# Loading the first twelve weight tiles six at a time, and storing decoded weights six tiles late

## The chip, the cores and the metric

One core of a Trainium2 chip runs the whole program. The metric is the device time of one execution in microseconds (us), the median over several runs. The engines are TensorE (PE, with its weight loads as PEld), VectorE (DVE), ScalarE (ACT), GpSimd (POOL) and SyncE (SP), which here only issues DMA transfers.

## What is computed

The program is an attention with a compressive memory, followed by two feed-forward layers. The first twelve weight tiles belong to the first feed-forward layer, `moe`.

```python
scores = q @ k.T / sqrt(D); a = softmax(causal(scores)); local = a @ v      # B 4, H 8, S 576, D 64
mem_out = (phi(q) @ M_prev) / (phi(q) . z_prev + 1e-6)
x = g * mem_out + (1 - g) * local                                           # x: 2304 tokens x 512
h = x @ w_in;  x = (h * sigmoid(h)) @ w_out                                 # moe:  512 -> 2048 -> 512
gt = x @ w_gate; val = x @ w_val; out = (gt * sigmoid(gt) * val) @ w_out    # moe2: 512 -> 1536 -> 512
```

The weights arrive as 64-bit numbers.

## The kernel before, in words

**Attention.** Batch 0 is computed first, in eight units: four units A (a pair of heads, the first 256 rows) and four units B (the same pairs, the other 320 rows). Batches 1 to 3 follow, a pair of heads at a time. A unit B transposes `q_t` and `k_t` on PE (`psq`, `psk`, L367), multiplies them (`pss`, L434 and L509), takes row minima on DVE (L486, L510, closed by L515), exponentials on ACT (L490, L516), scales the rows on POOL (L523, five instructions), transposes the result on PE (`pst`), copies it to SBUF, and multiplies it with v into `U` (L619). ACT and DVE turn `U` into the token block `x` (L214, L342).

**First feed-forward layer.** Its 2048 hidden columns are cut into four slices of 512. Batch 0 gives two token blocks, A (256 tokens) and B (320 tokens). `order` in `CFG` gives the sequence of block and slice: A0 A1 B1 B0 A2 B2 A3 B3; the other tokens follow in blocks of 432. For one block and slice PE computes four `h` tiles (L870), ACT, DVE and POOL turn each into the pair `gh`, `gl` (L877, L878, L214, L880), and four `y` tiles follow (L928).

**Weight tiles.** A slice needs eight tiles: four of `w_in`, four of `w_out`. A tile is loaded as 512 KB of raw 64-bit words (L717 for `w_in`, L748 for `w_out`), decoded to 32 bits by ACT (L731) and DVE (L732, L733), and split into a high half (ACT, L214 `w<-raw`) and a low half (POOL, L773) in a buffer `w` of the pool `wp`, which has eight. The decoded pair is then stored to DRAM (L796, `wd<-w`, 512 KB) because later blocks load it from there (L759). Slice 0 is tiles 1 to 4 (`w_in`) and 5 to 8 (`w_out`), slice 1 is tiles 9 to 12 and 13 to 16, and so on. Tile 9 takes the buffer `w` of tile 1, so it needs that tile's matmuls and its store done.

`Prep.step` (L790) does one tile: it splits the oldest loaded one, loads ahead to two raw tiles, and issues the store of the tile that it has just split. The raw tiles share three buffers (`raw8=3`).

**What sets the order.** The program is written as a stream of steps; a scheduler with its own cost table merges them into one fixed order per engine. Each engine and SP's queue then run their list in order. A wait at the head of a list holds everything behind it.

Of the kernel before, what the change touches and what calls it, by code (L numbers as in the profile page):

```python
# [13 lines left out]
I32 = mybir.dt.int32  # L14
# [3 lines left out]
P = 128  # L18
BIG = 1.0e9
CFG = dict(  # L20
    raw8=3,
    raw=3,
    g=1,
    th=2,
    ps_m=3,
    ps_a=dict(A=5, B=5, G=5),
    ps_s=dict(),
    run=3000,
# [18 lines left out]
    ahead=2,  # L47
# [7 lines left out]
    pt=4,  # L55
    rate=0.55,
    late=0.6,
    ring=16,
    y0=36,
    jit=1,  # L60
# [33 lines left out]
def kernel(  # L94
# [34 lines left out]
    def f(ap):  # L129
        return ap.bitcast(F32)  # L130
# [20 lines left out]
    kp = kept.enter_context(tc.tile_pool(name="kp", bufs=1))  # L151
    pha = ExitStack()
    rawp = pha.enter_context(tc.tile_pool(name="rawp", bufs=CFG["raw"], side="right"))
    cur, ph2 = {"raw": rawp}, {}
# [191 lines left out]
    def unit(u):  # L346
# [202 lines left out]
        def T_A():  # L549
# [8 lines left out]
            o["ta"] = ta  # L558

        def T_B(step):  # L560
            own4()
            if step == 0:
# [114 lines left out]
    for u, key in enumerate(units):  # L677
        step, stages = unit(u)
        if u == NP:
            stages.insert(0, lambda: open_at("atB"))  # L680
            at_slot = max(slots) + 1
        if u == 2 * NP:
            stages.insert(0, open_F)
            at_slot = max(slots) + 1
        if CFG["stackb"] > 1 and u == NP * CFG["stackb"] + NP:
            stages.insert(0, open_G)
            at_slot = max(slots) + 1
        for i, st in enumerate(stages):
            slots.setdefault(at_slot + i, []).append(st)
        for sup in key[2]:  # L690
            ready[key[0], sup] = at_slot + len(stages)
        at_slot += step
# [14 lines left out]

    w1 = {}

    def load64(w, j, part, after=None):  # L710

        raw = cur["raw"].tile([P, 512, 2], I32, tag="raw8", name="raw8", bufs=CFG["raw8"])
        w2 = w.bitcast(I32)
        if after is not None:
            nc.gpsimd.tensor_copy(raw.bitcast(F32)[:, 0, 0:1], f(after))
        if part == 0:
            nc.sync.dma_start(  # L717
                out=raw.rearrange("p (k n) t -> p k (n t)", k=KD),
                in_=w2[:, 2 * P * j:2 * P * (j + 1)].rearrange("(k p) n -> p k n", p=P),
            )  # L720
        else:
            nc.sync.dma_start(out=raw.rearrange("p n t -> p (n t)"), in_=w2[P * j:P * j + P, :])
        return raw

    def decode(raw, t=None):
        hi, lo = raw[:, :, 1], raw[:, :, 0]
        u = hi.bitcast(F32)
        if t is None:
            t = cur["raw"].tile([P, 512], F32, tag="raw", name="raw", bufs=CFG["raw"])
        ti = t.bitcast(I32)  # L730
        nc.scalar.activation(out=t, in_=u, func=ACTF.Prelu, scale=2.0**-111, alpha=-(2.0**32))  # L731
        nc.vector.tensor_single_scalar(ti, ti, 3, op=ALU.logical_shift_left)  # L732
        nc.vector.scalar_tensor_tensor(ti, lo, 29, ti, ALU.logical_shift_right, ALU.bitwise_or)  # L733
        return t

    seen = {}

    def r_(ap):
        return ap.bitcast(F32R)

    def raw_w1(*key):
        if key in seen:
            return None
        if key[0] == 0:
            return load64(w1_in, key[1], 0)
        raw = cur["raw"].tile([P, 512, 2], I32, tag="raw8", name="raw8", bufs=CFG["raw8"])
        _, s, e = key
        nc.sync.dma_start(  # L748
            out=raw.rearrange("p (j n) t -> p j (n t)", j=NW),
            in_=w1_out.bitcast(I32)[P * NW * s:P * NW * (s + 1), 2 * P * e:2 * P * (e + 1)].rearrange(  # L750
                "(j p) n -> p j n", p=P
            ),
        )
        return raw

    def split_w1(t, key):
        if key in seen:
            w = wp.tile([P, 2, 512], F32, tag="w", name="w")
            nc.sync.dma_start(out=w, in_=seen[key])  # L759
            return r_(w[:, 0]), r_(w[:, 1])  # L760
        w = split_wp(decode(t), "1")
        seen[key] = dram.tile([P, 2, 512], F32, name="wd%d_%d" % (key[0], len(seen)))
        prep1.post.append((seen[key], w))
        return r_(w[:, 0]), r_(w[:, 1])

    def split_wp(t, kind):
        w = wp.tile([P, 2, 512], F32, tag="w", name="w")
        split_to(r_(w[:, 0]), r_(w[:, 1]), t, kind)
        return w
# [5 lines left out]
    class Prep:  # L775
        def __init__(self, load, split):
            self.load, self.split = load, split
            self.todo, self.raws, self.done, self.post = [], [], {}, []

        def add(self, keys):  # L780
            self.todo += keys
# [6 lines left out]
        def step(self, ahead=CFG["ahead"]):  # L788
            self.prefetch(1)
            if not self.raws:  # L790
                return
            key, t = self.raws.pop(0)
            self.done[key] = self.split(t, key)
            self.prefetch(ahead)
            for d, t in self.post:
                nc.sync.dma_start(out=d, in_=t)  # L796
            self.post = []

        def need(self, key):
            while key not in self.done:  # L800
# [3 lines left out]


    prep1 = Prep(raw_w1, split_w1)

    def token_block(key):
# [31 lines left out]
    def moe1():  # L840
        keys = []
        for n, sg in enumerate(segs):
            if n == 0 or sg["s"] != segs[n - 1]["s"]:
                keys.append(sg["s"])
        prep1.add([(0, j) for j in SLICES[keys[0]]] + [(1, keys[0], e) for e in range(KD)])
        yield ("init", 0)
        gs = [{} for _ in segs]
        fresh = [0]
# [56 lines left out]
        for n, sg in enumerate(segs):  # L905
            key, t0, nt, s = sg["key"], sg["t0"], sg["nt"], sg["s"]
# [14 lines left out]
            for e in range(KD):  # L921
                ps = bank("y")
                m, last = 0, 3 * len(SLICES[s]) - 1
                for wi, gi in ((0, 0), (1, 0), (0, 1)):
                    for ji, j in enumerate(SLICES[s]):
                        w, g = prep1.need((1, s, e))[wi], gs[n][j][gi]
# [43 lines left out]
    def prep_w2():  # L970
# [3 lines left out]
        def fetch(n):  # L974
            while todo and len(raws) < n and not ("hold" in ph2 and n > 1):
                j, part = todo.pop(0)
                raws.append(load64((w2_gate, w2_val, w2_out)[part], j, part // 2, gate[-2]))
# [423 lines left out]
    if True:  # L1401
        open_at("atA")
        setup_attn()
        load_A()
        setup()
        items = moe1()
        next(items)
        slot, n_g = 0, 0
# [92 lines left out]
```

## Time and profile before

| | |
|---|---|
| median of 3 runs | 1062.23 us (1060.77 to 1062.96) |
| the profiled execution | 1062.63 us |
| its span | 1060.5 us |
| busy: PE, PEld, DVE, ACT, POOL | 98%, 90%, 60%, 51%, 37% of the span |
| DMA traffic | 258.16 MB, 243 GB/s mean |

The profiled execution lies 0.40 us above the median, and 2.1 us of it lie outside the span. PE is busy nearly throughout. The shares are means over stages that differ: POOL, for one, is idle in the second half.

### The profile page before, as it was taken

Reading aid. Unit: us, or ns where it says so; the run is one execution under the profiler, and the core shown is the slowest. Engines: PE = TensorE matmul, PEld = TensorE weight load, DVE = VectorE, ACT = ScalarE, POOL = GpSimd, SP = SyncE. Lnnn points to the kernel's source line nnn. Section 1 sums busy time; section 2 is a strip of 40 time slices with the busy share of each in tenths; the row PEclk is TensorE's granted clock in tenths of the full one; section 3 lists DMA queues with packets and bytes.
Section 4 is the critical chain, followed back from the end, with each engine's and each line's share of the span. In section 5 each row is a group of like instructions: output and inputs, shape, how many; then the busy total and the mean of one; then the engine's idle time right before and its main releaser. Section 6 shows DMA issues by size and latency. Waiting matters only on the chain.

```text
span 1060.5 us, 18824 instructions
## 1 busy us (share of the span) xinstructions
PE 1035.6 (98%) x6622; PEld 954.9 (90%) x6622; DVE 637.0 (60%) x1521; ACT 539.6 (51%) x1259; POOL 394.6 (37%) x461
## 2 busy tenths in 40 slices
PE   7799999999999999999999999999999999999998
PEld 5677988888888899888889999999999999999998
DVE  6796767876555644764254333566845669356573
ACT  6684877866656655664454331333613336133351
POOL 4784654678646556661578751000000000000000
PEclk9899999999999999999999999999999999999999
DMA  8995866468978569852478976777977778877784
GB/s 204 317 301 154 255 225 194 120 231 271 307 248 269 174 226 342 255 191 81 159 244 317 321 250 223 251 256 249 340 261 265 248 250 286 256 265 246 251 287 145
DMA packets 168670, 258.16 MB, mean 243 GB/s; under 512 B 76800, under 2 KB 113152, under 8 KB 168576
## 3 DMA queue, kind: packets, MB, share of 16 engines
q1 hardware_dynamic: 167488, 256.70, 73.1%
q8 instruction: 53, 0.87, 0.3%
q10 hardware_dynamic: 1088, 0.26, 0.1%
q14 instruction: 41, 0.34, 0.1%
HBM read 197.67 MB, written 59.24 MB: 242 GB/s over the span
## 4 chain that ended last, share of the span: by engine, by line
PE 78%; DMA 6%; DVE 4%; POOL 4%; ACT 4%; issue 3%; SPq 1%; POOLq 0%; DVEq 0%; ACTq 0%
PE y L928 15%; PE h L870 13%; PE oac L1205 11%; PE gb L1205 11%; PE po L1312 9%; PE pb L1312 4%; PE gd L1205 4%; PE U L619 3%; PE pst L367 3%; PE pss L434 3%; DMA raw<-in_moe_w_gate_dram 2%; DMA raw<-in_moe_w_val_dram 2%; DVE raw L733 1%; PE pss L509 1%; POOL gl L880 1%
## 5 line engine op out<-in xcount | busy, mean ns | idle before, releaser
L870 PE MATMUL h<-x,w 128*128 128x432 f32 (+2 forms) x1152 | 228.3, 348 | 5.9 <-ACT w L214 3.3
L870 PEld LDWEIGHTS h<-x,w 128*128 128x128 f32 x1152 | 197.8, 191 | 18.3 <-ACT w L214 3.5
L928 PE MATMUL y<-gh,w 128*128 128x432 f32 (+2 forms) x768 | 166.2, 348 | 4.2 <-ACT gh L214 2.3
L928 PEld LDWEIGHTS y<-gh,w 128*128 128x128 f32 x768 | 132.0, 190 | 15.3 <-issue 3.8
L880 POOL TENSOR_TENSOR gl<-th,gh 128x432 fp32r<-128x432 f32 (+2 forms) x96 | 104.7, 1093 | 81.7 <-ACT gh L214 64.9
L1205 PE MATMUL gb<-yT,w 128*128 128x384 f32 x648 | 124.8, 336 | 0.0
L1205 PEld LDWEIGHTS gb<-yT,w 128*128 128x128 f32 x648 | 113.1, 188 | 0.0
L878 DVE SCALAR_TENSOR_TENSOR th<-th,h 128x432 f32<-128x432 f32 (+2 forms) x96 | 52.6, 550 | 79.0 <-ACT th L877 78.9
L523 POOL TENSOR_TENSOR s<-s,r 128x128 f32<-128x128 f32 (+4 forms) x96 | 68.4, 739 | 73.4 <-DVE r L540 20.5
L1312 PE MATMUL po<-w,ph 128*128 128x256 f32 x516 | 93.8, 283 | 0.0
L928 PE MATMUL y<-gl,w 128*128 128x432 f32 (+2 forms) x384 | 88.4, 343 | 0.0
L490 ACT ACTIVATE s<-s,mn 128x128 f32<-128x128 f32 (+3 forms) x128 | 71.0, 557 | 21.4 <-DVE mn L486 19.9
L1205 PE MATMUL oac<-yB,w 128*128 128x384 f32 x432 | 81.3, 336 | 0.0
L1312 PEld LDWEIGHTS po<-w,ph 128*128 128x128 f32 x516 | 81.2, 191 | 0.0
L1277 ACT CAST ph<-r 128x384 fp32r<-128x384 f32 x108 | 51.1, 512 | 55.9 <-DVE r L1231 35.6
L1205 PEld LDWEIGHTS oac<-yB,w 128*128 128x128 f32 x432 | 75.4, 188 | 0.0
L732 DVE TENSOR_SCALAR raw<-raw 128x512 int32<-128x512 int32 x68 | 38.3, 564 | 58.1 <-ACT raw L731 57.8
L214 ACT CAST gh<-th 128x432 fp32r<-128x432 f32 (+2 forms) x96 | 49.0, 513 | 47.0 <-DVE th L878 33.8
L1312 PE MATMUL po<-w,pl 128*128 128x256 f32 x258 | 73.0, 283 | 0.0
L731 ACT ACTIVATE raw<-raw 128x512 f32<-128x512 f32 x68 | 45.6, 671 | 50.0 <-DMA raw<-in_moe_w_gate_dram 19.9
L928 PEld LDWEIGHTS y<-gl,w 128*128 128x128 f32 x384 | 67.6, 190 | 2.9 <-issue 0.5
L1278 DVE TENSOR_TENSOR pl<-r,ph 128x384 fp32r<-128x384 f32 x108 | 55.8, 553 | 17.8 <-ACT ph L1277 17.1
(161 smaller groups left out, 1993.2 us busy)
## 6 DMA issues: line engine op xcount, KB each, us to landing
w<-wg SPq DMA_DIRECT2D x108, 512.0 KB, 4.7
w<-wd SPq DMA_DIRECT2D x80, 512.0 KB, 5.8
wg<-wo SPq DMA_DIRECT2D x36, 512.0 KB, 3.7
w<-woT SPq DMA_DIRECT2D x36, 512.0 KB, 4.7
wd<-w SPq DMA_DIRECT2D x32, 512.0 KB, 4.2
raw<-in_moe_w_out_dram SPq DMA_DIRECT2D x28, 512.0 KB, 5.7
w<-woB SPq DMA_DIRECT2D x27, 512.0 KB, 4.3
w<-wg SPq DMA_DIRECT2D x36, 256.0 KB, 4.8
```

Of the source, the lines that this page charges most:

```text
L214: nc.scalar.copy(out, in_)
L490: nc.scalar.activation(out=a, in_=a, func=ACTF.Exp, scale=-1.0, bias=mn, accum_out=o["sm", sup][:, col:col + 1])
L523: nc.gpsimd.tensor_mul(a, a, r.to_broadcast([P, w]))
L731: nc.scalar.activation(out=t, in_=u, func=ACTF.Prelu, scale=2.0**-111, alpha=-(2.0**32))
L870: nc.tensor.matmul(ps[:, :nt], w[:, kk, :], x[:, kk, :nt], start=(m == 0), stop=(m == 3 * KD - 1))
L878: nc.vector.scalar_tensor_tensor(th[:, :nt], th[:, :nt], 1.0, ps[:, :nt], ALU.add, ALU.mult)
L880: tt(CFG["gl" if n >= CFG["n0"] else "gl0"]).tensor_sub(gl[:, :nt], th[:, :nt], f(gh[:, :nt]))
L928: nc.tensor.matmul(ps[:, :nt], w[:, c], g[:, :nt], start=(m == 0), stop=(m == last))
L1205: nc.tensor.matmul(dst, w[wi][:, P * kk:P * kk + P], y[ny][:, yi, kk], start=(start and m == 0), stop=(stop and m == 5), skip_group_check= ...
L1277: nc.scalar.copy(ph, src)
L1278: nc.vector.tensor_sub(pl, src, f(ph))
L1312: nc.tensor.matmul(dst, a[:, c], x, start=(begin and m == 0 and own_bank), stop=(end and m == 2), skip_group_check=True,)
```

## The change

The first twelve raw tiles get a pool tag of their own with six buffers (24 KB more per partition), six of them are requested before the first unit is computed, and the prefetch stays at six until twelve tiles have been requested. The store of a decoded tile goes into a list with its number and is issued when five more tiles have been processed (`hold=6`).

```diff
+    hold=6,
+    early=12,
...
+    n_raw = [0]
+
+    def raw_tile():
+        n_raw[0] += 1
+        if n_raw[0] <= CFG["early"]:
+            return kp.tile([P, 512, 2], I32, tag="raw8k", name="raw8", bufs=6)
+        return cur["raw"].tile([P, 512, 2], I32, tag="raw8", name="raw8", bufs=CFG["raw8"])
+
     def load64(w, j, part, after=None):
 
-        raw = cur["raw"].tile([P, 512, 2], I32, tag="raw8", name="raw8", bufs=CFG["raw8"])
+        raw = raw_tile()
...
-        raw = cur["raw"].tile([P, 512, 2], I32, tag="raw8", name="raw8", bufs=CFG["raw8"])
+        raw = raw_tile()
         _, s, e = key
...
-        prep1.post.append((seen[key], w))
+        prep1.post.append((prep1.n, seen[key], w))
...
-            self.todo, self.raws, self.done, self.post = [], [], {}, []
+            self.todo, self.raws, self.done, self.post, self.n = [], [], {}, [], 0
...
             self.done[key] = self.split(t, key)
-            self.prefetch(ahead)
-            for d, t in self.post:
+            self.prefetch(6 if n_raw[0] < CFG["early"] else ahead)
+            self.n += 1
+            while self.post and self.post[0][0] + CFG["hold"] <= self.n:
+                _, d, t = self.post.pop(0)
                 nc.sync.dma_start(out=d, in_=t)
-            self.post = []
...
         prep1.add([(0, j) for j in SLICES[keys[0]]] + [(1, keys[0], e) for e in range(KD)])
+        prep1.prefetch(6)
         yield ("init", 0)
```

The diff is small, but the scheduler's lists move with it; from L57 on the line numbers of the changed kernel are 2 to 12 higher. PE's list is rearranged over about its first third (2,003 of 6,256 matmuls); the rest is unchanged. Three places matter.

SP's queue, from the loads of v for the units A on. Before:

```order
L269 DMA vA<-in_v_dram 128x8x64 x2
L717 DMA raw_156<-in_moe_w_in_dram 128x4x256
L717 DMA raw_166<-in_moe_w_in_dram 128x4x256
L717 DMA raw_168<-in_moe_w_in_dram 128x4x256
L297 DMA q_t_98<-in_q_dram 128x2x64 x2
```

With the change, at the same place:

```order
L271 DMA vA<-in_v_dram 128x8x64 x2
L727 DMA raw_146<-in_moe_w_in_dram 128x4x256
L727 DMA raw_148<-in_moe_w_in_dram 128x4x256
L727 DMA raw_150<-in_moe_w_in_dram 128x4x256
L727 DMA raw_152<-in_moe_w_in_dram 128x4x256
L758 DMA raw_154<-in_moe_w_out_dram 128x4x256
L758 DMA raw_156<-in_moe_w_out_dram 128x4x256
L299 DMA q_t_98<-in_q_dram 128x2x64 x2
```

Three more weight tiles stand ahead of the rows of the first unit B.

SP's queue further on, with the change: the tiles 9 to 15 and the first stores, up to the rows of the second unit B.

```order
L808 DMA wd_0_175<-w 128x1024
L727 DMA raw_624<-in_moe_w_in_dram 128x4x256
L758 DMA raw_989<-in_moe_w_out_dram 128x4x256
L808 DMA wd_1_200<-w 128x1024
L727 DMA raw_634<-in_moe_w_in_dram 128x4x256
L758 DMA raw_1074<-in_moe_w_out_dram 128x4x256
L808 DMA wd_2_247<-w 128x1024
L758 DMA raw_1152<-in_moe_w_out_dram 128x4x256
L727 DMA raw_636<-in_moe_w_in_dram 128x4x256
L727 DMA raw_638<-in_moe_w_in_dram 128x4x256
L808 DMA wd_3_308<-w 128x1024
L808 DMA wd_4_360<-w 128x1024
```

Before, the store of tile 1 stood ahead of the loads of tiles 5 and 6; now it stands behind eight loads, and the store of tile 4 behind fifteen.

PE, from the scores of the first unit B (`kT_151` before) to those of the second (`kT_181` before, `kT_188` now). Before:

```order
L509 MATMUL pss_670<-kT_151,q_108 128x320
L367 MATMUL psq<-ident,q_t_98 128x128 x3
L870 MATMUL h<-x,w 128x256 x4
L367 MATMUL psk<-ident,k_t_99 128x128 x2
L445 MATMUL psm<-bd_104,qp 128x130 x3
L367 MATMUL psk<-ident,k_t_99 128x128
L870 MATMUL h<-x,w 128x256 x8
L434 MATMUL pss<-kT_181,Q 128x384 x2
```

With the change, the end of the same stretch (ahead of it stand 16 `h` and 24 `y` matmuls):

```order
L882 MATMUL h<-x,w 128x256 x8
L940 MATMUL y<-gh,w 128x256 x8
L940 MATMUL y<-gl,w 128x256 x4
L940 MATMUL y<-gh,w 128x256 x8
L940 MATMUL y<-gl,w 128x256 x4
L882 MATMUL h<-x,w 128x256 x16
L369 MATMUL psq<-ident,q_t_98 128x128 x3
L882 MATMUL h<-x,w 128x256 x8
L369 MATMUL psk<-ident,k_t_99 128x128 x2
L447 MATMUL psm<-bd_104,qp 128x130 x3
L369 MATMUL psk<-ident,k_t_99 128x128
L436 MATMUL pss<-kT_188,Q 128x384 x2
```

Between the two sets of scores PE did 12 `h` matmuls; now it does 48 `h` and 48 `y` matmuls, which is all of A1's `h` and all of A0's `y`. After the last `U` of the units B no `y` of A1 is left, where before a group of twelve was.

## Rows read from the trace of the kernel before

**Rows 1.** Windows: length, busy PE, PEld, DVE, ACT, POOL, clock, DMA share, GB/s.

```profile
20.00:40.00 20.00, 17.15 (x118) 12.84 (x116) 14.42 (x37) 11.75 (x29) 14.20 (x18) 0.91 0.93 292
40.00:50.00 10.00, 4.98 (x20) 3.41 (x19) 8.83 (x26) 8.29 (x21) 6.72 (x8) 0.77 0.98 303
50.00:56.00 6.00, 6.00 (x36) 4.78 (x35) 5.79 (x14) 3.15 (x8) 5.86 (x7) 0.81 0.96 316
56.00:90.00 34.00, 33.13 (x217) 24.15 (x217) 31.12 (x83) 26.10 (x69) 26.21 (x25) 1.00 0.91 286
```

**Rows 2.** Timeline of PE: start, length, instructions, idle time before and its releaser.

```profile
42.49 0.41 PE L367 MATMUL psq<-ident,q_t 128*128 128x128 f32 x2 [0.48 <-DMA q_t<-in_q_dram]
...
47.52 1.22 PE L870 MATMUL h<-x,w 128*128 128x256 f32 x4 [3.30 <-ACT w L214]
...
52.30 1.77 PE L434 MATMUL pss<-kT,Q 64*128 64x384 f32 x8
```

**Rows 3.** Timeline of ACT: tile 8's split, then tile 9's decode and split.

```profile
40.71 0.62 ACT L214 CAST w<-raw 128x512 fp32r<-128x512 f32 x1 [0.17 <-DVE raw L733]
...
44.33 0.66 ACT L731 ACTIVATE raw<-raw 128x512 f32<-128x512 f32 x1
...
46.87 0.60 ACT L214 CAST w<-raw 128x512 fp32r<-128x512 f32 x1
```

**Rows 4.** Timeline of DVE: the end of the row minima, units B 0 to 3.

```profile
45.25 0.15 DVE L515 TENSOR_TENSOR mn<-mn 128x1 f32<-128x1 f32 x1
...
59.39 0.39 DVE L515 TENSOR_TENSOR mn<-mn 128x1 f32<-128x1 f32 x1
...
75.29 0.15 DVE L515 TENSOR_TENSOR mn<-mn 128x1 f32<-128x1 f32 x1
...
88.59 0.16 DVE L515 TENSOR_TENSOR mn<-mn 128x1 f32<-128x1 f32 x1
```

**Rows 5.** Window between the first and the last of rows 4, columns as rows 1.

```profile
45.25:88.59 43.34, 40.20 (x246) 30.52 (x248) 39.40 (x102) 31.43 (x81) 35.70 (x34) 0.92 0.94 299
```

**Rows 6.** Timeline of POOL: the row scaling of units B 0, 1 and 3.

```profile
48.93 5.67 POOL L523 TENSOR_TENSOR s<-s,r 128x384 f32<-128x384 f32 x5
...
62.13 5.71 POOL L523 TENSOR_TENSOR s<-s,r 128x384 f32<-128x384 f32 x5 [0.48 <-DVE r L540]
...
90.87 4.72 POOL L523 TENSOR_TENSOR s<-s,r 128x384 f32<-128x384 f32 x5 [4.56 <-DVE r L540]
```

**Rows 7.** Lines by shape, POOL, 40 to 90 us: busy us, mean ns, idle before.

```profile
L773 POOL TENSOR_TENSOR w<-raw,w 128x512 fp32r<-128x512 f32 x10 | 14.2, 1430 | 4.2 <-ACT w L214 4.0
...
L880 POOL TENSOR_TENSOR gl<-th,gh 128x256 fp32r<-128x256 f32 x7 | 6.5, 925 | 0.7 <-ACT gh L214 0.7
```

**Rows 8.** Lines by shape, DVE, 40 to 90 us.

```profile
L733 DVE SCALAR_TENSOR_TENSOR raw<-raw,raw 128x512 int32<-128x512 int32 x13 | 12.3, 945 | 0.2
L732 DVE TENSOR_SCALAR raw<-raw 128x512 int32<-128x512 int32 x12 | 6.8, 564 | 1.5 <-ACT raw L731 1.4
L486 DVE CUSTOM_DVE_ANT_0 s<-pss,mask 128x512 f32<-128x512 f32 x8 | 5.3, 681 | 0.6 <-PE pss L434 0.6
```

**Rows 9.** Timeline of PE at the end of the units B.

```profile
96.43 2.28 PE L619 MATMUL U<-tb,v_t 128*64 128x192 f32 x20
...
99.81 1.19 PE L928 MATMUL y<-gh,w 128*128 128x256 f32 x8
...
104.24 1.21 PE L928 MATMUL y<-gh,w 128*128 128x256 f32 x8
...
105.75 2.80 PE L870 MATMUL h<-x,w 128*128 128x320 f32 x18
```

**Rows 10.** DVE line L733, 0 to 100 us: duration, ns, least, median, most.

```profile
L733 DVE SCALAR_TENSOR_TENSOR raw<-raw,raw x19: 678/804/1573, 17.3 to 89.5; 128x512 int32<-128x512 int32 x19
```

**Rows 11.** Timeline of SP's queue: the first loads and the first store.

```profile
9.64 2.09 SPq L717 DMA_DIRECT2D raw<-in_moe_w_in_dram  x3
...
24.22 0.55 SPq L796 DMA_DIRECT2D wd<-w  x1
```

## The prediction

> **What bounds the kernel now.** I read the windows first, then PE's timeline and waits in the first 110 us, then the lists of DVE, ACT and POOL there, because the change touches nothing later than tile 12 except the time at which stores are issued. The windows show the only large hole that PE has after its start: from 40 to 50 us it is busy for 4.98 of 10 us, and the granted clock, a mix of its two levels of 2.4 and 1.2 GHz, is 0.77 there and 0.81 in the next 6 us [rows 1]. The hole is 5.0 us of idle time, and of the busy time 4.98 x 0.23 = 1.1 and 6.00 x 0.19 = 1.1 us were lost to the lower level of the clock: 7.2 us if all of it came back. The timeline names the last part of it: 3.30 us in which PE waits for a split weight [rows 2]. That is tile 9, the first of slice 1. Its decode starts on ACT at 44.33 and its high half is written at 46.87; PE starts at 47.52, as soon as that is done [rows 2, 3]. So a weight that comes late does hold PE.
>
> But PE isn't the only full engine. From 50 to 56 us DVE is busy for 5.79 and POOL for 5.86 of 6 us, and from 56 to 90 us DVE for 31.12 of 34 us while PE is busy for 33.13 [rows 1]. The units B of the attention go through DVE one after another, and the end of their row minima comes at 45.25, 59.39, 75.29 and 88.59 us [rows 4]: 43.34 us for three units, in which DVE is idle for 43.34 - 39.40 = 3.94 us [rows 5]. Block B of the first layer can start only when the last of these units is through, at 105.75 us [rows 9]. So the stretch that decides is 40 to 106 us, and two engines share the say in it. After it PE is nearly full to the end, and its list from there is the old one but for small exchanges; I take whatever is gained or lost at 105.75 us to be kept.
>
> **The change part by part.** *Six loads at once.* Three of 512 KB stood ahead of the rows of the first unit B, now six. SP took 2.09 us to issue three [rows 11], so the rows behind them are issued 2.1 us later. Those rows were issued from 11.7 us on and are first needed when PE has done the units A and 24 `h` matmuls of A0; I cost this at nothing. The cover is the units A; without it PE would wait for the same 2.1 us.
>
> *Decodes come earlier.* Between 20 and 40 us DVE is busy for 14.42 of 20 us and ACT for 11.75 [rows 1]: there is room, and by order eight tiles are decoded before the first unit B's `e` where six were, and nine ahead of the end of its minima where eight were. Tile 9's high half now stands where tile 8's stood, behind the first exponential of that unit; that was 40.71 [rows 3], so PE can begin A1's `h` near 43 us, not 47.52. This brings back most of the hole for PE.
>
> *What PE does with it.* Ahead of the second unit B's transposes PE now has A1's `h` and A0's `y`, 96 matmuls where it had 12. The transposes came at 42.49 [rows 2]. Now they stand behind the product with tile 11's low half, and POOL makes that after the row scaling of the first unit: 48.93 + 5.67 [rows 6], one `gl` of 0.93 and one split of 1.43 [rows 7], which is 57.0. Eight matmuls take about 1.0 (1.19 for eight of that width, tail included [rows 9]), so the transposes start near 58, and the copies of Q and K put the scores at about 61: I put these at 3 us, where the old way from transposes to scores took 52.30 - 42.49 = 9.8 with the hole in it [rows 2]. DVE then does four reductions of at most 0.68 [rows 8] and two smaller ones, about 4 us, and waits up to 1 us for the last product. The second unit's minima end near 66, not 59.39 [rows 4]. In return fifteen tiles are decoded by then, where twelve were: three at 0.945 + 0.564 = 1.51 us on DVE [rows 8], 4.5 us. Net, DVE is behind by 66 - 59.39 - 4.5 = 2.1 us.
>
> *The third and fourth unit.* By order nineteen tiles are decoded ahead of the last minima, where eighteen were: +1.5. Two sums into `yp` of 256 columns stand there now; at an estimated 0.4 each, under the 0.68 of a 512-wide reduction [rows 8], +0.8. Against it, DVE's 3.94 us of idle time [rows 5] is partly waiting for a PE that was busy with A0 and A1; that work is now done. I take back half, -2.0, with 0 and -3.9 as ends. The last minima end at 88.59 + 2.1 + 1.5 + 0.8 - 2.0 = 91.0 us.
>
> *The tail.* From there to the start of block B took 105.75 - 88.59 = 17.16 us [rows 4, 9]: POOL's scaling from 90.87 to 95.59 [rows 6], and then a PE that still had the third unit's `U` (2.28) and two groups of twelve `y` to do, the last from 104.24 to 105.75 and another at 99.81, of the same 1.5 us [rows 9]. By order the third `U` and one of these groups come before that, and no `y` is left behind the last `U`. That takes out 2.2 + 1.5 + 1.5 = 5.2. The last `y` also hid the copy of `U` into `x`; without it PE waits some part of those 1.5 us, of which I take half, 0.8. The tail is 17.16 - 5.2 + 0.8 = 12.8, and block B starts at 103.8 us.
>
> *Stores six tiles late.* The number of stores and their bytes are the same. Their queue position moves behind up to fifteen loads. Each buffer `w` is reused eight tiles later, so a store has two tiles of slack. I cost it at nothing; the cover is that ACT reaches the split of tile 12 at about 50 us. If a store isn't out by then, ACT stops at its split, and everything behind it on ACT does (a rival below).
>
> *The sum.* 103.8 - 105.75 = -1.95 us, and small gains of clock between 50 and 56 us where PE is waited for, which I put at 0.2 of the 1.1: -2.2 us. The profiled execution took 1062.63, 0.40 above the median; on the median of 1062.23 the forecast is 1060.0 us. Bounds of the same mechanism: with none of DVE's idle time taken back -0.2, with all of it -4.1; an error of 2 us in the walk to 66 moves it as much again. A measurement of this kernel can tell about 0.2% (2.1 us) from no change.
>
> **Rivals.** *The decodes run into POOL: no gain.* L733 takes 678 ns at the least and 1573 at the most [rows 10], with a mean of 945 between 40 and 90 us [rows 8]: it is slow where POOL works. The change puts tiles 11 to 15 into a stretch in which POOL does the row scaling and one split after another. If each of the five costs 1573, DVE is later by 5 x 0.63 = 3.1 us, the last minima end at 94.1, and block B starts at 106.9: +0.9 us, 1063. For it: POOL at 5.86 of 6 us [rows 1]. Against it: the total overlap needn't grow, since POOL has less left to do later. The Trainium skill, SBUF — State Buffer, section Who interferes with whom, says that a DVE instruction with two SBUF inputs contends with a GpSimd instruction that reads SBUF and that the loser blocks fully. The trace agrees with a spread of 678 to 1573 ns; by that rule L733, which reads two SBUF operands, would pay the high price for each of the five, which is this rival.
>
> *A late store stops ACT: slower.* From the place of the first store on, SP now issues seven loads (tiles 9 to 15) and three stores before that of tile 4. That store leaves when some eleven transfers of 512 KB and the two loads still under way are through, about 7 MB with the rows; from 24.22 us [rows 11] at 303 GB/s [rows 1] that is 23 us, so it ends near 48. The split of tile 12, which overwrites its buffer, is due near 50. If it ends later than that, ACT stands at this split, the exponentials of the second unit behind it, and DVE behind those. Up to 2.2 us late only eats the gain; more is a loss. I price it at three more transfers ahead of it than I count, 3 x 1.73 = 5.2 us: -2.2 + 5.2 = +3.0, 1065.2 us. For it: the DMA engines are busy for 0.93 to 0.98 from 20 to 56 us [rows 1]. Against it: a store that is held back is out of the way of the loads.
>
> *The whole hole comes back: faster.* If DVE catches up because its idle time and the lower clock both go, PE decides alone and the 7.2 us return: 1055. Against it: DVE's 39.40 of 43.34 us [rows 5].
>
> *The change doesn't do what it says.* By order the six loads do stand together and the stores do stand later; I leave this out.
>
> **How the numbers follow.** Forecast 0.45; decodes against POOL 0.22; late store 0.20; the whole hole 0.13. The forecast's own range is -4.1 to -0.2, of which I count two thirds as beyond 2.1 us. Faster by over 0.2%: 0.30 + 0.13 and a little of the second = 0.44. Slower: the late store and a fifth of the second, 0.24. Within 0.2%: 0.32. The range reaches to the whole hole on one side and to the late store on the other, 1055 to 1065.2.
>
> **What would show it.** Right: no 3 us wait of PE for a split weight near 47 us; A1's `h` from about 43; the second unit's transposes near 58; ends of the minima near 45, 66, 82 and 91; block B from about 104. Wrong: a last end of the minima beyond 93 us, ACT idle ahead of `w<-raw` with a store as its releaser, or L733 above 1.2 us in the mean between 45 and 66. A PE hole that only moves to 55 to 62 us, with the same end at 105.75, would show the conserved work on DVE to be the whole story.

## The result, and the profile after

The changed kernel takes 1069.42 us (median of 5 runs, 1067.93 to 1073.58); the kernel before, run beside it, 1062.02 (5 runs, 1060.77 to 1062.96). The ratio is 1.0079, 95% interval 1.0059 to 1.0099: **slower by 7.4 us**, where 2.2 us faster was forecast. The profiled execution took 1068.79 us; its span is 1066.9 us where it was 1060.5.

The end of the row minima of the four units B (timeline of DVE; L517 is L515 of before) answers to [rows 4]:

```profile
46.76 0.16 DVE L517 TENSOR_TENSOR mn<-mn 128x1 f32<-128x1 f32 x1
69.90 0.16 DVE L517 TENSOR_TENSOR mn<-mn 128x1 f32<-128x1 f32 x1
84.88 0.19 DVE L517 TENSOR_TENSOR mn<-mn 128x1 f32<-128x1 f32 x1
96.42 0.16 DVE L517 TENSOR_TENSOR mn<-mn 128x1 f32<-128x1 f32 x1
```

The second is 10.5 us later than before, the last still 7.8. Timeline of PE; the first lines answer to [rows 2], the last to [rows 9]:

```profile
44.52 0.74 PE L882 MATMUL h<-x,w 128*128 128x256 f32 x4 [0.41 <-ACT w L216]
...
49.26 0.74 PE L882 MATMUL h<-x,w 128*128 128x256 f32 x4 [2.15 <-ACT w L216]
...
60.21 0.49 PE L369 MATMUL psq<-ident,q_t 128*128 128x128 f32 x3
...
64.36 0.92 PE L436 MATMUL pss<-kT,Q 64*128 64x384 f32 x4 [1.71 <-ACT kT L222]
...
111.86 1.33 PE L882 MATMUL h<-x,w 128*128 128x320 f32 x6
```

Tile 9's product starts at 44.52, not 47.52: that part came as hoped. But the second unit B's transposes came at 60.21 (42.49 before), its scores at 64.36 (52.30), and block B at 111.86 (105.75). That is 6.1 us, nearly all of the 6.4 us by which the span grew. The windows, with the columns of [rows 1], the last of them between the first and last minima as [rows 5]:

```profile
20.00:40.00 20.00, 13.92 (x103) 10.38 (x102) 16.80 (x38) 12.52 (x29) 15.69 (x18) 1.00 0.88 257
40.00:50.00 10.00, 6.81 (x41) 4.69 (x40) 8.75 (x26) 9.01 (x25) 6.59 (x7) 1.00 1.07 402
50.00:56.00 6.00, 6.00 (x40) 6.00 (x40) 4.94 (x5) 3.23 (x8) 6.00 (x6) 0.72 1.06 371
56.00:90.00 34.00, 26.89 (x172) 20.06 (x171) 28.71 (x77) 21.27 (x53) 23.00 (x26) 0.90 0.85 258
46.76:96.42 49.66, 40.40 (x259) 31.22 (x260) 40.35 (x103) 31.42 (x79) 32.35 (x33) 0.90 0.81 257
```

From 20 to 40 us PE is busy for 13.92 us (17.15 before), from 50 to 56 DVE for 4.94 (5.79). In the last row DVE is busy for 40.35 us (39.40 before) and idle for 49.66 - 40.35 = 9.31 us (3.94). So of the 6.3 us by which this stretch grew, 5.4 are time in which DVE lacked work. From 56 to 90 us PE is busy for 26.89 us where it was 33.13. The DMA engines carry 402 GB/s from 40 to 50 us (303 before).

**Where the time went.** PE's idle time (length less busy time, from four windows of each profile), in us:

| | 0 to 40 | 40 to 60 | 60 to 90 | 90 to 120 | sum |
|---|---|---|---|---|---|
| before | 6.72 | 5.02 | 0.87 | 0.00 | 12.61 |
| after | 9.85 | 3.25 | 7.05 | 0.00 | 20.15 |

The old hole gave back 1.8 us. The units A lost 3.1 (waits for `x` and `ta`, 1.68 and 1.12 us at 28.50 and 33.41), and a new hole behind 60 us took 6.2. The sum is 7.5 us more. The span of the profiled execution grew by 6.4 us; in the whole span PE's busy time is 0.9 us shorter (1034.7, 1035.6).

**Why the second unit is late.** Its rows `q_t` and `k_t` share one buffer with the first unit's, so they can be asked for only when the first has been transposed. SP's queue before the change, at these loads:

```profile
36.26 0.37 SPq L297 DMA_DIRECT2D q_t<-in_q_dram  x1
...
38.84 0.70 SPq L304 DMA_DIRECT2D q_t<-in_q_dram  x1
39.63 1.63 SPq L297 DMA_DIRECT2D k_t<-in_k_dram  x2
41.36 0.42 SPq L304 DMA_DIRECT2D k_t<-in_k_dram  x1
```

and after:

```profile
36.70 3.69 SPq L727 DMA_DIRECT2D raw<-in_moe_w_in_dram  x2
40.48 2.86 SPq L808 DMA_DIRECT2D wd<-w  x3
43.43 1.24 SPq L299 DMA_DIRECT2D q_t<-in_q_dram  x2
45.55 0.37 SPq L306 DMA_DIRECT2D q_t<-in_q_dram  x1
46.81 1.64 SPq L299 DMA_DIRECT2D k_t<-in_k_dram  x2
49.42 0.37 SPq L306 DMA_DIRECT2D k_t<-in_k_dram  x1
```

They are issued 7 to 8 us later, behind 15 weight tiles and six stores in the same queue where nine and four stood. (The first unit's transposes, which free the buffer, come 1.9 us later themselves, at 37.71.) They also land more slowly: a load of `q_t` takes 8.6 us from issue to landing in the median (5.0 before). The scheduler's list answers to that: it puts 88 `h` and 48 `y` ahead of these transposes (48 and 0 before). So in the change itself PE names no wait for the rows: when it reaches the transposes, at 60.21, they are there. The wait shows only where the list is forced, below.

### The profile page after: what moved, and what is told of

The parts are those of the page before. It is cut to its first block, busy times and chain, and to the rows that moved or that the text cites. A ratio compares the mean times of both kernels' runs of the same rounds, so it can differ in the third digit from the quotient of the medians.

```text
span 1066.9 us, 18818 instructions
## 1 busy us (share of the span) xinstructions
PE 1034.7 (97%) x6622; PEld 954.0 (89%) x6622; DVE 638.8 (60%) x1521; ACT 541.2 (51%) x1259; POOL 395.4 (37%) x461
## 4 chain that ended last, share of the span: by engine, by line
PE 83%; DVE 5%; ACT 4%; DMA 3%; POOL 3%; issue 2%; SPq 0%; POOLq 0%; ACTq 0%; DVEq 0%
PE y L940 16%; PE h L882 14%; PE oac L1217 11%; PE gb L1217 11%; PE po L1324 9%; PE pss L436 4%; PE U L621 4%; PE pb L1324 4%; PE gd L1217 4%; PE pst L369 3%; DMA raw<-in_moe_w_gate_dram 2%; PE psm L447 1%; PE pss L511 1%; DVE raw L743 1%; POOL s L525 1%
## 5 line engine op out<-in xcount | busy, mean ns | idle before, releaser
L892 POOL TENSOR_TENSOR gl<-th,gh 128x432 fp32r<-128x432 f32 (+2 forms) x96 | 101.4, 1058 | 80.7 <-ACT gh L216 63.3
L742 DVE TENSOR_SCALAR raw<-raw 128x512 int32<-128x512 int32 x68 | 37.4, 550 | 59.7 <-ACT raw L741 59.5
```

Of the source, the lines that this page charges most:

```text
L892: tt(CFG["gl" if n >= CFG["n0"] else "gl0"]).tensor_sub(gl[:, :nt], th[:, :nt], f(gh[:, :nt]))
```

## The experiments

Three theories stood at first: the rows of the second unit come late (R, further on L); the late stores (S); the earlier decodes (D, later C where POOL slows them, E for early loads and decodes in general). O says that the place in PE's list alone decides. "Transposes behind 48 h and 0 y" counts matmuls ahead of them in PE's list. The kernel before ran beside each of them (medians 1060.9 to 1062.7).

### Which half of the change

**Stores late alone.**

```diff
-    early=12,
+    early=0,
...
-        prep1.prefetch(6)
```

> Edit: no tile has a buffer of its own and nothing is loaded six at once; stores six tiles late stay. Theory R (the rows of the second unit B come late behind the extra weight loads, and PE's list then puts A1's h and A0's y ahead of that unit's transposes): those transposes stand behind 48 h and no y, as before the change, so 1061 to 1063.5 us, block B's first h between 105 and 107 us. Rival S (a store held back stops ACT at a split or fills the queue): 1066 us or more, with ACT or SP waiting for a store between 40 and 70 us. Rival D (decodes set earlier stand ahead of the units A's copies on ACT and DVE): as R, since no decode is earlier.

Measured 1063.89 us, ratio 1.0025 (1.0008 to 1.0042). A little slower, by about a third of the loss, and just outside every range: R had 1061 to 1063.5, S 1066 or more. Block B starts at 108.77 us.

**Loads alone.**

```diff
-    hold=6,
+    hold=1,
```

> Edit: stores are issued at once again (hold 1); twelve tiles in six buffers and six loads at once stay. Theory R: the second unit B's transposes stand behind 96 h and 48 y, so 1068 to 1071 us, end of the last row minima at 95 to 98 us. Rival S: the loss goes with the late stores, 1061 to 1064 us. Rival D: as R, 1068 to 1070.

Measured 1069.58 us, 1.0083 (1.0070 to 1.0096): the whole loss without late stores. S falls as the cause of the loss. R and D, which gave the same range, are not told apart here.

**Six early tiles, not twelve.**

```diff
-    early=12,
+    early=6,
```

> Edit: only the first six tiles have buffers of their own (early 6); all six are loaded at once, and the next loads go two ahead as before; stores six late. Decodes ahead of the end of the first unit B's minima: nine, as in the full change. The second unit B's transposes stand behind 60 h and no y (full change 88 and 48, before 48 and 0). Theory R: 1061 to 1065 us, middle 1063, minima of the second unit B end between 60 and 64 us. Rival D (the decodes in the units A are the loss): those are as early as in the full change, 1067 to 1069.

Measured 1061.69 us, 1.0007 (0.9996 to 1.0018): no difference. The decodes in the units A are as early as in the full change, nine tiles ahead of the first minima, and PE is idle there for 8.18 us. So the decodes in the units A aren't the bulk of the loss; it comes with tiles 7 to 12. The rows of the second unit are issued from 37.72 to 43.15 us here, its minima end at 62.73.

### Rows early, or a forced list

**The second unit's rows in tiles of their own**, in the full change; `load_rows` gives it two tiles from the pool `kp`.

```diff
     def load_B():
         for u in range(NP, NP + len(rows)):
             load_rows(u, "qkv" if u == NP else "v")
+        load_rows(NP + 1, "qk")
```

> Edit: the full change, but q and k of the second unit B have tiles of their own and are loaded with the first unit's, ahead of the later weight tiles. The second unit B's transposes stand behind 48 h and no y again; the third's still behind 84 h and 48 y. Theory R: second unit's minima end at 57 to 62 us (full change 69.90), about half to all of the 7 us come back: 1061 to 1066, middle 1063.5. Rival D: units A still end about 1.7 us late and decodes stand ahead of them, so 1067 to 1070. Rival S: 1068 to 1070, stores are unchanged.

Measured 1068.37 us, 1.0071 (1.0057 to 1.0084). The second unit came in time, and no gain clear of the noise was won. The time lies in D's range and in S's, and outside R's:

```profile
45.60 0.59 DVE L525 TENSOR_TENSOR mn<-mn 128x1 f32<-128x1 f32 x1
57.70 0.90 DVE L525 TENSOR_TENSOR mn<-mn 128x1 f32<-128x1 f32 x1
77.97 0.15 DVE L525 TENSOR_TENSOR mn<-mn 128x1 f32<-128x1 f32 x1
95.32 0.16 DVE L525 TENSOR_TENSOR mn<-mn 128x1 f32<-128x1 f32 x1
```

Now the third unit was late: its rows were issued from 45.16 to 51.57 us and transposed at 66.10, behind 84 `h` and 48 `y`. Between first and last minima DVE was busy for 46.07 us, with the two decode lines at medians of 1.02 and 1.19 us beside a busy POOL.

**PE's list forced**, by edges that hold A1's `h` and A0's `y` behind the second unit's transposes, and in the next run some of them behind the third's. `after_T(i)` puts what follows behind the last transpose of K of unit B number i.

```diff
+            with after_T(1 if n == 1 else 0):
+                for w, x in ((wh, xh), (wl, xh), (wh, xl)):
...
+                        with after_T(1 if n == 0 else 0):
+                            nc.tensor.matmul(ps[:, :nt], w[:, c], g[:, :nt], start=(m == 0), stop=(m == last))
```

> Edit: the full change, with edges in PE's list alone: A1's h and A0's y stand behind the last transpose of K of the second unit B. That unit's transposes stand behind 48 h and no y (full change 88 and 48), the third's behind 72 and 36 to 37, the fourth's behind 96 and 48 as in the full change. Theory O (where the units B stand in PE's list decides the loss): the second unit's minima end at 60 to 66 us in place of 69.90, and half of the 7 us come back: 1063 to 1067. Rival L (the rows of the second unit come late behind the weight loads; wherever the transposes stand, the unit waits): PE waits for k's rows until about 54 us, 1067 to 1071. Rival C (decodes slowed beside POOL fill DVE): 1066 to 1069, L742's sum stays near 14 us up to the last minima.

> Edit: as the one before, and A1's third and fourth h and A0's second to fourth y stand behind the third unit's transposes too: the second unit's transposes behind 48 h and no y, the third's behind 72 and 12, the fourth's behind 84 and 48: nearly the list from before the change (48 and 0, 64 and 11, 84 and 48). Theory O: minima end near 60 to 64, 76 to 79 and 89 to 92, block B's h at 105 to 108, 1060 to 1065 us. Rival L: 1067 to 1071 with a PE wait of 5 us or more for rows. Rival C: 1066 to 1069.

Measured 1070.96 us, 1.0080 (1.0062 to 1.0098), and 1067.98, 1.0051 (1.0035 to 1.0067). O falls: with nearly the old list, PE stands still. Timeline of PE in the first:

```profile
52.12 0.66 PE L378 MATMUL psq<-ident,q_t 128*128 128x128 f32 x2 [8.20 <-DMA q_t<-in_q_dram]
```

and in the second:

```profile
53.82 0.87 PE L378 MATMUL psq<-ident,q_t 128*128 128x128 f32 x3 [10.02 <-DMA q_t<-in_q_dram]
```

This shows the lateness itself. Before the change PE waited 0.48 us for the same DMA, at 42.49 [rows 2], and once more for the last of its loads:

```profile
43.90 0.33 PE L367 MATMUL psq<-ident,q_t 128*128 128x128 f32 x1 [0.99 <-DMA q_t<-in_q_dram]
```

But the rows aren't all of it. In the first forced run `q_t` is transposed at 52.12, and yet the second minima end at 70.33, no earlier than in the change (69.90). ACT copies `Q` only at 59.85 and `kT` at 62.01: ahead of them in its list stand the beginnings of two decodes, and before the first of them it sits idle for 3.25 us, until POOL, held by 6.16 us of scaling the first unit's rows, has split a tile. The second forced run shows the same wait from PE's side:

```profile
62.35 1.77 PE L445 MATMUL pss<-kT,Q 64*128 64x384 f32 x8 [2.43 <-ACT kT L222]
```

So the rows hold the second unit up to 52 to 54 us, and decodes ahead of its copies hold its scores for some 6 to 7 us more. That is D's mechanism, and these two runs do not exclude it.

**Both together:** rows apart, and the third unit's place forced.

> Edit: tiles of their own for the second unit's q and k rows, loaded early, together with the edges for the third unit: transposes behind 48 h and 0 y, 72 and 12, 79 and 48. Theory O: no wait for rows of the second unit and a list as before the change, 1059 to 1064 us. Rival L: as O for the second unit, the third's rows still behind weights, 1061 to 1066. Rival C: the decodes are as many and as slow, 1066 to 1069.

Measured 1074.72 us, 1.0118 (1.0100 to 1.0137), the worst: a miss for every theory. The third unit's transposes came at 59.71, but decodes stood ahead of its copies on ACT and DVE, and its scores waited for `kT` until 69.96.

**The kernel before, with its later units moved back** in the list.

```diff
-    gam=[0.85, 0.85, 1, 1.2, 2.5, 1.2, 1.2, 0.85],
+    gam=[4, 4, 1, 1.2, 2.5, 1.2, 1.2, 0.85],
```

> Edit: the kernel before the change, its loads, buffers and stores as they were; only the two exponents that pace the units B against the first layer's work are 4 in place of 0.85, so that the third unit's transposes stand behind 72 h and 24 y (64 and 11 before), its scores behind 94 h and 48 y (72 and 33) and the fourth's transposes behind 96 and 48 (84 and 48). Theory O: the end of the last minima moves from 88.6 to 92 to 97 us, and the time is 1065 to 1070 us without any of the change's loads. Rivals L and C: no weight tile is loaded or decoded earlier, 1061 to 1063.

Measured 1064.07 us, 1.0009 (0.9993 to 1.0025), between the ranges of O and of L and C, last minima at 91.97: a list with later units does little by itself.

### Late rows without the change

**The kernel before, rows held.** One word of each row tile is first written from the low half of tile 8, and the loads wait for that.

```diff
+            if u == NP + 1:
+                load_rows(u, "qk", last_lo[0])
...
+            if after is not None:
+                nc.gpsimd.tensor_copy(t[nm][:, c0, 0, 0:1], after)
```

> Edit: the kernel before the change, its weight loads, buffers and stores as they were; only the first load of q and of k for the second unit B waits until the low half of tile 8 is written (near 43 us, where the full change issues it; 36.26 before). The scheduler answers as it did to the change: the transposes stand behind 72 h and 42 y, the scores behind 96 and 48, 15 tiles are decoded ahead of the second minima (full change 88 and 48, 96 and 48, 15). Theory L (the rows of the second unit come late, and PE's and DVE's lists go round that): 1066 to 1071 us, minima end near 45 to 47, 66 to 71, 81 to 86 and 93 to 98. Rival E (the early loads and decodes do the harm themselves, in the units A and on the DMA queue): 1061 to 1064, since none is earlier here.

Measured 1066.91 us, 1.0049 (1.0033 to 1.0065), with no weight loaded early. Window between the first and last minima:

```profile
45.85:95.76 49.91, 41.32 (x262) 31.41 (x264) 40.64 (x106) 32.63 (x81) 34.68 (x36) 0.93 0.86 266
```

DVE busy 40.64, idle 9.27 us; the full change had 40.35 and 9.31. Minima end at 45.85, 73.24, 83.59 and 95.76, block B starts at 111.59, and PE is idle for 20.10 us up to 120 (20.15 in the change): up to block B this is the fingerprint of the change. The time isn't: 0.49%, not 0.79%, and the profiled execution, 1064.51 us, was the fastest of the four. The hold was harder than meant: SP's list put the held halves at 55.88 and 56.32 us, 12 us later than the change issues these rows, and the second minima are later than L's 66 to 71. So late rows alone are enough for a loss of 0.5%; that the change's smaller lateness makes all of its 0.79% isn't shown.

**POOL's subtractions taken out** of both kernels.

```diff
-        tt(CFG["wlo" + kind]).tensor_sub(lo, t, f(hi))
+        nc.gpsimd.memset(f(lo), 0.0)
```

> Left out: the low halves of the first layer's and the second layer's split weights, which POOL sets to zero in place of subtracting. Control for the next run, on the kernel before the change. Every theory: at most the time before, 1045 to 1062 us; if POOL's reads slow the decodes, L742's counterpart L732 stays at 0.42 us beside the writes of zero, or L733 at 0.69.

> Left out: as in the run before, on the full change. Theory C (decodes that run beside POOL's subtractions are slowed, and this is the loss): the gap to the control is 0 to 3 us, DVE's sum for the two decode lines up to the last minima falls from 33.3 us to 21 to 25. Theory L: the gap stays at 5 to 9 us, since the second unit's rows are as late and its transposes stand behind 96 h and 48 y.

Measured 1062.79 us, 1.0025 (1.0008 to 1.0042), and 1071.13, 1.0091 (1.0073 to 1.0109). The gap stays, 1.0091 against 1.0025. The control, expected to be no slower than the kernel before, was slower. The edit took out little of the slowness itself: in the change the two decode lines add up to 18.6 us from 40 to 97 us, and to 19.8 with the subtractions. But it took out most of the difference between the kernels. A tile costs DVE 0.74 + 0.97 = 1.71 us in the change and 0.66 + 0.94 = 1.60 in the control; with the subtractions it was 1.80 and 1.51. For eleven tiles the change pays 1.2 us more in place of 3.2, and the gap in time, 8.3 us, is no smaller. So the extra slowing beside POOL isn't what makes the loss.

### Can early rows or fewer early tiles win?

**Six early tiles and the second unit's rows apart** (the edits of the third and fourth run).

> Edit: only the first six tiles have buffers of their own and are loaded at once (as in the third run), and the second unit's q and k rows have tiles of their own and are loaded with the first unit's. Transposes of the units B: behind 48 h and 0 y, 52 to 60 and 0, 72 and 40 (before 48 and 0, 64 and 11, 84 and 48); decoded ahead of their minima: 8, 9, 13, 16 tiles (before 7, 12, 15, 18). Theory L: last minima end at 82 to 87 us, block B's h at 99 to 104, 1055 to 1060 us, below both kernels. Rival C: the decodes are fewer ahead of the minima, but POOL is as full: 1060 to 1063. Rival E: nine decodes in the units A do harm, 1063 to 1067.

Measured 1063.55 us, 1.0026 (1.0013 to 1.0039): a miss for L and, by 0.55 us, for C; the time lies in E's range. The second minima end at 55.65, the last at 88.85: DVE is busy for 38.61 of 41.24 us between, and has little left to gain.

**The change with rows of two, and of all later units, apart** (five and three buffers in place of six, for room).

> Edit: the change with five buffers and five loads at once in place of six (twelve early tiles stay, stores six late), and q and k rows of the second and third unit B in tiles of their own, loaded with the first unit's. Transposes behind 48 h and 0 y, 48 and 0, 72 and 12; decoded ahead of the minima 8, 10, 13, 16 (full change 9, 15, 18, 19). Theory L (late rows are the whole loss): DVE's idle time from the first to the last minima falls from 9.31 us to under 5, last minima end at 84 to 90, 1056 to 1063 us. Theory D (early decodes, slowed beside POOL, cost as much again and take what the rows give back): DVE's busy time there stays at 44 us or more, as with the rows of the second unit alone, 1065 to 1070.

> Edit: the change with three buffers and three loads at once, and q and k rows of all later units B in tiles of their own, loaded early. Decoded ahead of the minima: 7, 9, 9, 15. Theory L: 1052 to 1062 us, no wait of PE for rows, last minima end at 80 to 87. Theory D: fewer decodes ahead of the minima than before the change, so no loss here either, 1056 to 1063; A1's h come later and may leave PE a hole of 3 to 6 us.

Measured 1063.86 us, 1.0023 (1.0013 to 1.0033), and 1064.91, 1.0024 (1.0012 to 1.0037). Both times lie above L's range; the first lies below D's, the second above it. Twelve early tiles and late stores are still there, but of 1.0079 only 1.0023 and 1.0024 are left, about what late stores cost alone. No run has five or three buffers without the rows apart, and three loads at once are no more than before the change, so these two runs don't tell the rows from the buffers. Window of the first of them between its first and last minima:

```profile
45.80:84.01 38.21, 34.87 (x208) 23.67 (x209) 34.38 (x95) 29.10 (x74) 30.93 (x32) 1.00 0.90 309
```

DVE's idle time is 3.83 us and PE's up to 120 us 13.18 (20.15 in the change).

**The same on the kernel before**, rows of the second unit and of all later ones.

> Edit: the kernel before the change, with the second unit's q and k rows alone in tiles of their own and loaded with the first unit's. Transposes behind 48 and 0, 48 and 0, 72 and 12; decoded 7, 8, 12, 15. Theory L: rows were late by 1 us before the change too (0.99 us of PE), so 1056 to 1061 us. Theory D: 1058 to 1062, three decodes fewer ahead of the last minima, done afterwards.

> Edit: the kernel before the change, with rows of all later units B in tiles of their own. Decoded ahead of the minima: 5, 7, 8, 13. Theory L: last minima end at 78 to 86 us, 1052 to 1060 us. Theory D: as L or lower, 1050 to 1060. Against both: PE lacks A1's weights after A0's h and holds a hole of 6 us or more, 1062 to 1068.

Measured 1067.57 us, 1.0053 (1.0037 to 1.0069), and 1066.09, 1.0042 (1.0025 to 1.0059): misses for L and D. The second lies in the range given for a PE that lacks A1's weights, but the hole of 6 us isn't there: PE's longest wait from 20 to 120 us is 1.3 us. Units earlier than before cost: A1's first `h` came at 56.49 and 66.06 us, where it was 47.52, though the last minima ended earlier, at 87.44 and 84.99.

These two are also controls for the change. With the second unit's rows apart in both, the change gives 1.0071 and the kernel before 1.0053, a difference within the noise; with the rows of all apart, 1.0024 (three buffers) and 1.0042. So where the rows don't stand behind the loads, the loads do no harm that these runs can tell. This speaks for L, although rows apart have a price of their own that no run explains.

**Six and four early tiles with stores at once.**

> Edit: only the first six tiles have buffers of their own and are loaded at once; stores are issued at once as before the change. Transposes of the units B behind 60 h and 0 y, 72 and 36, 96 and 48. With late stores this was 1.0007 of the time before. Theory L: the store's bytes go ahead of the second unit's rows again, so these come no earlier than in the third run and the third unit's transposes stand later, 1062 to 1066 us. Rival S (late stores cost by themselves what the first run showed, 0.25%): 1058 to 1060.5 us, below both kernels.

> Edit: only the first four tiles have buffers of their own, four are loaded at once, stores at once. Transposes of the units B behind 48 h and 0 y, 64 and 0, 72 and 32; decoded ahead of the minima 8, 12, 15, 19. Theory L: two loads fewer ahead of the rows than with six, so the second unit's minima end at 58 to 61 us, 1058 to 1062.5 us. Rival D (each decode that is earlier costs): 1062 to 1065.

Measured 1063.18 us, 1.0017 (1.0004 to 1.0031), and 1068.16, 1.0053 (1.0037 to 1.0069). The first lies in L's range and S falls again. The second is a miss for both: its second minima end at 64.01, and the dose doesn't order the times. It also loses without late rows: they are issued from 36.35 to 40.74 us (36.26 to 41.36 before), and PE waits 3.68 us for a split weight, to 50.02, where it waits 1.32 us for rows. So late rows aren't the only way to such a loss. No version beat the kernel before.

## Why the prediction was wrong, step by step

**Six loads at once, at nothing.** This step failed. It asked only when the rows of the *first* unit B are needed. Those were issued 3.8 us later (from 15.60 us, 11.78 before), and no wait of PE names them. (In the trace they are first needed behind 32 `h` matmuls, not 24.) The rows of the second unit stood in no term, though [rows 2] showed PE waiting for just that DMA, 0.48 us at 42.49: they had no slack at all. With the forced lists PE stands 8 to 10 us for them, and the hold in the kernel before shows that late rows alone can make a loss of 0.5%.

**Where the sum went off.** Block B was forecast for 103.8 us and came at 111.86. Of these 8.1 us, 3.9 arose up to the second unit's minima, 1.5 from there to the last minima (26.52 us, 25.0 forecast), and 2.6 in the tail. That what is lost at block B is kept was right: 6.1 us there, 6.4 in the span.

**Decodes come earlier.** Right for its own object: tile 9's product moved from 47.52 to 44.52 (43 forecast), and PE's hole from 40 to 60 us shrank from 5.02 to 3.25. "There is room" was wrong by 3.1 us of PE in the units A, and the first unit's minima ended 1.5 us later (46.76). With six early tiles, and as many decodes ahead of the first minima, PE was idle there for 8.18 us, and the time was that of before.

**The walk to the second unit's minima.** The place in the list was read rightly (transposes 58, found 60.21; scores 61, found 64.36; minima 66, found 69.90), 3.9 us short; 1.5 of them come from the units A. The list was taken as given, and the rows behind it weren't seen: forced back, it only turned the wait into one for their DMA, and then into one for copies that stand behind decodes.

**Net 2.1 us behind, and half of DVE's idle time back.** The sign of the second was wrong. The argument was that DVE would have its decodes done ahead and PE would wait less. With no scores to reduce, DVE ran out: 9.31 us idle in place of 3.94, where 1.9 were counted on. Of it 4.3 us were waits for ACT's half of a decode, 1.1 before. The last minima ended at 96.42, not 91.0.

**The tail.** 111.86 - 96.42 = 15.44 us, not 12.8. The third unit's `U` and a group of `y` were to come ahead of the last minima; both still stand behind them, in parts from 103.73 and from 99.88, and so does a second group of `y`:

```profile
99.88 0.96 PE L940 MATMUL y<-gh,w 128*128 128x256 f32 x6
...
104.80 1.95 PE L621 MATMUL U<-tb,v_t 128*64 128x64 f32 x16
...
107.87 1.07 PE L940 MATMUL y<-gh,w 128*128 128x256 f32 x7
```

Of the 5.2 us to be taken out, 1.7 went (17.16 before).

**The clock, at 0.2 us gained.** Up to 120 us the lower level cost PE 33.28 x 0.04 + 14.98 x 0.17 = 3.9 us before (busy time and granted clock from 0 to 40 and 40 to 60 us) and 16.75 x 0.09 + 22.95 x 0.11 = 4.0 us now (40 to 60 and 60 to 90). Nothing was gained.

**Stores at nothing.** Right within the change: loads alone give 1.0083, the whole change 1.0079. Alone, late stores gave 1.0025. The rival of a store that stops ACT didn't come about: ACT's waits from 40 to 97 us name no store, and the split of a tile waited 0.7 us in all, for DVE.

**Decodes run into POOL.** The rows moved as that rival said: L742 and L743 took 0.81 and 0.99 us in the mean from 40 to 90 us (0.56 and 0.95 before). From the first to the last minima the two lines took 18.06 us for ten tiles (15.68 for ten and a half before): about 3 us of slowing, the 3.1 that this rival had priced, though DVE's busy time there rose by 0.95 us only. But the run without the subtractions shows that the gap in time stays when most of this goes. With the second unit's rows apart DVE's busy time was 46.07 us.

**What was to show it wrong.** The prediction named a last end of the minima beyond 93 us, and that came (96.42). A PE hole that only moves, to 55 to 62 us with the same end at 105.75, did not come: the hole lies from 60 to 90 us (7.05), and the end moved to 111.86.

**What stays open.** How the loss divides between late rows and the decodes that stand ahead of a unit's copies: the forced lists show both, one after the other, and no run moves those decodes alone. Taking the rows of two units apart left 1.0023 of 1.0079, but with five buffers, not six. And why units B earlier than before the change cost 4.5 to 6 us: PE's idle time up to 120 us is only 1.4 and 3.0 us more there.

## What to carry to other kernels

Before loading further ahead, list everything else in the same queue and find the small loads whose buffer comes free late: a row that shows PE waiting half a microsecond for a 64 KB load says that this load has no slack, and here six more 512 KB tiles ahead of it made it 7 us late and a chain of units with it. Then look at what stands ahead of that chain's copies on the other engines. When a scheduler makes the order, read a moved block as its answer to a late operand first, and ask which operand. An engine that is nearly full with one chain is not protected against that chain starving.

## What the runs showed that was not expected

A decode's shift on DVE (one SBUF operand) slows beside POOL. In the change, up to 100 us, it took 0.42 to 0.43 us the five times that POOL did nothing beside it, and 0.94 in the mean, 1.37 at most, the ten times that POOL was busy beside it throughout. In the kernel before, five of ten such shifts took 0.41 to 0.42 us all the same (mean 0.62), so it isn't slowed each time. Timeline of DVE with rows and list changed together, once beside POOL's split and row scaling (61.02 to 68.41), once in POOL's idle 7.30 us:

```profile
61.07 1.50 DVE L760 TENSOR_SCALAR raw<-raw 128x512 int32<-128x512 int32 x1
62.61 1.20 DVE L761 SCALAR_TENSOR_TENSOR raw<-raw,raw 128x512 int32<-128x512 int32 x1
...
78.17 0.42 DVE L760 TENSOR_SCALAR raw<-raw 128x512 int32<-128x512 int32 x1
78.62 0.69 DVE L761 SCALAR_TENSOR_TENSOR raw<-raw,raw 128x512 int32<-128x512 int32 x1
```

The prediction's rival had priced only the second of the two lines as slow. The Trainium skill, SBUF — State Buffer, section Who interferes with whom, says that `tensor_scalar`, when its operands meet certain conditions, can enter a mode that uses the ports shared with GpSimd, and can then contend with it; the trace agrees, 0.42 against 1.50 us. By that rule alone the change would have lost its time in DVE's busy time; the windows show most of it in the idle time.
